# Attention weights moved in two transfers from 64 partitions to 128 rows in place of four from 32 to 64

## The chip, the cores and the metric

The kernel runs on one core of one Trainium2 chip. A time is the device time of one execution in microseconds, and the metric is the median over runs of the same kernel. Beside the runs there is one profiled execution, whose records give the durations used below.

## What is computed

The inputs are q, k and v of 8 batches, 8 heads, 576 positions and a head size of 64, a threshold `tau`, and the weights of a feed-forward layer. Everything is float32 for the attention; the feed-forward weights arrive as 64-bit floating-point values, which the kernel converts itself. Cut to what matters:

```python
scores = scale * np.matmul(q, k.transpose(0, 1, 3, 2))
thresh = np.max(scores, axis=-1, keepdims=True) - tau
scores = np.where(scores >= thresh, scores, -1000000000.0)
attn = softmax(scores)
x = np.matmul(attn, v)                      # then (B,H,S,D) -> (B*S, H*D)
h = x @ w_in
solu = h * softmax(h)
ln = (solu - mean(solu)) / np.sqrt(var(solu) + 1e-06) * g_ln
out = ln @ w_out
```

`x` has 4608 rows of 512, `h` 1024 columns.

## The kernel before

The work of the attention is cut into slots of 128 query rows for each of two heads. A slot is written (b, kind, hp, r): batch, kind, pair of heads, and half r. Kinds 0 and 1 are the two halves of the first 512 positions, kind 2 the last 64 positions of all four pairs. Two slots, r = 0 and r = 1, are a unit; there are 8 x 2 x 4 = 64 units of kinds 0 and 1 and 8 of kind 2, 72 in all, of 144 slots.

The program is one hand-written loop of rounds (L839 to L984), one slot a round, with an order for each engine that is exactly the order of the calls. In a round:

- TensorE makes the scores of the slot in PSUM, two heads side by side (`scores`, L451). VectorE takes the row minimum of the negated scores (`maxes`, L473), ScalarE applies threshold and exponential (`ramp` L488, `exps` L497), GpSimd normalises the rows one round later (`normalise`, L504 to L507).
- VectorE then transposes the weights in blocks of 32x32 into T (`blocks`, L519). The block of 32 query rows number R (0 to 3) of a slot lies in T's partitions 32 R to 32 R + 31, and a partition there stands for key position mod 32. T has two buffers.
- After the second slot of a unit SyncE's queue issues the block transfers (L530). They turn T into wT, where 64 partitions hold 64 key positions (the block column's half c is folded into the partition: source partition j gives target rows 2j and 2j + 1), so that TensorE can contract over keys. wT has two buffers and a part g of its free dimension.
- About three rounds later (`LAG_PV`, L750) TensorE multiplies v with wT: 72 matmuls a unit of kinds 0 and 1, on 64-row halves u of wT and of v (`attend_steps`, L555). ScalarE copies the sum from PSUM to xh, in the order of tokens (`attended`, L578).
- The feed-forward part of earlier tokens fills the rest of each round: `ff_h` (L611), `ff_max`, `ff_exp`, `ff_mul`, `ff_stats`, `ff_norm` and `ff_norm2` on the other engines, then `ff_swap` (four transfers V<-u on SyncE's queue, L693), the transpose `ff_turn` (L703), `ff_o` (L715) and the store (L742).

SyncE's queue carries nearly all transfers, in the order in which the round issues them: V<-u of `ff_swap` ahead of wT<-T, then stores, the transposed k (kT<-flip, L194), and last the loads of q, k, v and, in the first 16 rounds, of the weights (`weight_load`, L248). The weight pieces are converted on VectorE (L259 to L282), ScalarE (L264, L298) and GpSimd (L292) in those rounds too.

In the kernel before, the transfers of a unit pair the quarter R = 2 half + g with target rows 64 half to 64 half + 63 and part g, and so the half u of TensorE's rows is R // 2 and the part g is R % 2:

```python
for g in range(2):
    for half in range(2):
        of = 64 * half + 32 * g
        nc.sync.dma_start(out=to[ROWS[half], g], in_=T[of : of + 32])
```

Of the kernel before, what the change touches and what calls it, by code (L numbers as in the profile page):

```python
# [16 lines left out]
P = 128  # L17
# [3 lines left out]
def kernel(  # L21
# [27 lines left out]
    nc = tc.nc  # L49
# [10 lines left out]
    ROWS = (slice(0, 64), slice(64, P))  # L60
# [35 lines left out]
    xh = {}  # L96
# [414 lines left out]
    def blocks(s):  # L511
        b, kind, hp, r = slots[s]
        key = (b, kind, hp)
        if r == 0:
            units[key] = dict(T=work.tile([P, NB, 2, 2, 32], F32, tag="T", name="T"))
        u = units[key]
        T = u["T"]
        for h, w in enumerate(live.pop(s)["w"]):
            nc.vector.transpose(out=T[:, :, r, h, :], in_=w)  # L519
        if r == 0:  # L520
            return


        T = T.rearrange("p (c m) r h x -> p c (m r h x)", c=2)
        u["wT"] = wT = work.tile([P, 2, NK, 2, 2, 32], F32, tag="wT", bufs=2, name="wT")
        to = wT.rearrange("p g m r h x -> p g (m r h x)")
        for g in range(2):
            for half in range(2):
                of = 64 * half + 32 * g
                nc.sync.dma_start(out=to[ROWS[half], g], in_=T[of : of + 32])  # L530
# [31 lines left out]
    def attended(key):  # L562
        b, kind, hp = key
        tag, y = units.pop(key)["y"]
        y = y.rearrange("p (u n) -> p u n", u=2)[:, :, 0:P].rearrange("p u (r y) -> p u r y", r=2)
        if kind == 2:
            if b % 2 == 0:
                xe[b // 2] = work.tile([P, NP, P], F32, tag="xe", bufs=1, name="xe")
            to = xe[b // 2][:, :, 64 * (b % 2) : 64 * (b % 2) + 64].rearrange(
                "p (u r) y -> p u r y", u=2  # L570
            )
        else:
            if hp == 0:
                xh[b, kind] = work.tile(
                    [P, NP, 256], F32, tag=f"xh{(2 * b + kind) % 4}", bufs=1, name="xh"
                )
            to = xh[b, kind][:, hp].rearrange("p (r u y) -> p u r y", r=2, u=2)
        nc.scalar.copy(out=to, in_=y)  # L578
        pairs_free.append(tag)

# [181 lines left out]
    for i in range(NP, NPAIR):  # L762
        b, hp = divmod(i, NP)
# [27 lines left out]
    for i in range(2 * NP, NPAIR):  # L791
        b, hp = divmod(i, NP)
# [16 lines left out]
    with tc.manual_schedule():  # L809
# [29 lines left out]
        while True:  # L839
# [29 lines left out]
            if more:  # L869
# [3 lines left out]
                while preps and preps[0][0] <= rnd and preps[0][1] <= room:  # L873
                    _, n, make, _ = preps.pop(0)
# [80 lines left out]
            if attending is not None:  # L955
                for _ in beside or attend_steps(attending):
                    pass
                attended(attending)
                b, kind, hp = attending
                if kind == 2 and b % 2:  # L960
                    ready.append((rnd + 1, [(b // 2,)]))
                elif kind < 2 and hp == NP - 1:
                    ready.append((rnd + 1, [(b, kind, 0), (b, kind, 1)]))
            if rnd - 1 in live:
                blocks(rnd - 1)
# [6 lines left out]
            if rnd in pieces:  # L972
                x = pieces[rnd]
# [44 lines left out]
```

## Time and profile before

| | |
|---|---|
| median of 3 runs | 885.61 us (884.29 to 887.14) |
| profiled execution, its own time | 883.54 us |
| its span, first to last instruction | 881.8 us |
| granted TensorE clock, mean | 0.980 |
| TensorE busy | 835.4 us |
| wT<-T transfers | 288 of 288 KB, 5.9 us from issue to landing (median) |
| transfers in all | 161.60 MB, DMA engines busy 76.6% through SyncE's queue |
| eviction of pv to xh | 64 copies, 370 ns each |

The span is the time between the first and the last instruction of the program; 1.7 us of the execution lie outside it. The busy share of an engine is a mean over an opening, in which the weights are converted, a long middle of equal rounds, and an end in which only the feed-forward part runs.

### The profile page before, as it was taken

The page shows a single profiled execution, that of the slowest core. Times are in us where ns is not written, and L with a number is a line of the kernel's source. Part 1 is how long each engine was busy: PE and PEld are TensorE (multiplying, and loading weights), DVE is VectorE, ACT ScalarE, POOL GpSimd, SP SyncE. Part 2 cuts the span into 40 slices and gives each one's busy share as a digit, 9 for nine tenths or more (in the row PEclk, how much of TensorE's full clock was granted, in tenths as well). Part 3 has the DMA queues.
Part 4 walks back from the last instruction along what each step waited for, and adds up shares of the span by engine and source line. Part 5 has one row for each costly group of instructions (what it writes and reads, how often), then busy time and mean ns, then how long its engine had stood idle before and what let it go on. Part 6 is the DMA issues. An engine that isn't in the chain of part 4 may idle for free. (4 is left out here: it accounts for less than half of the span.)

```text
span 881.8 us, 38016 instructions
## 1 busy us (share of the span) xinstructions
PE 835.4 (95%) x16225; PEld 592.1 (67%) x16225; DVE 682.0 (77%) x1248; ACT 586.3 (66%) x1201; POOL 471.0 (53%) x888
## 2 busy tenths in 40 slices
PE   5667999989999999999999999999999999999997
PEld 3445666665676877677777777777677677777655
DVE  5989788878787888888778887888687888777451
ACT  5977777767666766767677677777676777775121
POOL 2878655545555555555554655555555555555120
PEclk9878899999999999999999999999999999999999
DMA  7999978887878796988789787888779777866222
GB/s 230 254 260 256 218 186 196 217 191 175 201 170 212 178 208 157 206 207 189 158 194 214 184 204 166 208 213 185 165 173 219 182 174 155 186 133 143 65 49 49
DMA packets 85033, 161.60 MB, mean 183 GB/s; under 512 B 19832, under 2 KB 49536, under 8 KB 84864
## 3 DMA queue, kind: packets, MB, share of 16 engines
q1 hardware_dynamic: 83728, 157.18, 76.6%
q8 instruction: 127, 2.08, 1.1%
q10 hardware_dynamic: 1136, 2.00, 0.7%
q14 instruction: 42, 0.34, 0.1%
HBM read 46.14 MB, written 9.44 MB: 63 GB/s over the span
## 5 line engine op out<-in xcount | busy, mean ns | idle before, releaser
L473 DVE CUSTOM_DVE_ANT_0 w<-s_ps,tau_t 128x576 f32<-128x576 f32 x280 | 200.7, 754 | 108.0 <-PE s_ps L451 90.7
L715 PE MATMUL o_ps<-w,uT 64*64 64x256 f32 x4608 | 265.2, 376 | 1.1 <-DVE uT L703 1.1
L488 ACT ACTIVATE w<-s_ps,nth 128x576 f32<-128x576 f32 x280 | 199.8, 743 | 97.0 <-DVE nth L473 93.1
L715 PEld LDWEIGHTS o_ps<-w,uT 64*64 64x64 f32 x4608 | 218.9, 133 | 58.3 <-issue 13.8
L507 POOL TENSOR_SCALAR w<-w,sm 128x576 f32<-128x576 f32 x288 | 218.8, 772 | 14.3
L497 ACT ACTIVATE w<-w,ntau 128x576 f32<-128x576 f32 x288 | 220.3, 772 | 0.0
L611 PE MATMUL h_ps<-w,xh 64*64 64x512 f32 x1856 | 220.0, 596 | 0.0
L519 DVE STREAM_TRANSPOSE T<-w 128x576 f32<-128x576 f32 x288 | 206.3, 752 | 7.4 <-POOL w L507 6.0
L555 PEld LDWEIGHTS pv<-wT,v 64*64 64x64 f32 x5760 | 166.5, 136 | 51.1 <-issue 36.3
L451 PE MATMUL s_ps<-kT,qT 64*64 64x64 f32 (+1 forms) x2048 | 168.1, 422 | 16.4 <-ACT w L488 12.5
L555 PE MATMUL pv<-wT,v 64*64 64x128 f32 (+1 forms) x5760 | 170.9, 263 | 7.9 <-DMA wT<-T 3.7
L611 PEld LDWEIGHTS h_ps<-w,xh 64*64 64x64 f32 x1856 | 98.3, 135 | 96.6 <-issue 88.6
L504 POOL TENSOR_SCALAR sm<-sm 128x2 f32<-128x2 f32 x144 | 36.0, 250 | 229.5 <-ACT w L497 226.4
L505 POOL TENSOR_TENSOR sm<-sm,mone 128x2 f32<-128x2 f32 x144 | 104.6, 726 | 12.0
L677 ACT ACTIVATE V<-u,nb,rs 128x1024 f32<-128x1024 f32 x36 | 44.7, 1241 | 52.2 <-POOL nb L667 52.2
L451 PEld LDWEIGHTS s_ps<-kT,qT 64*64 64x64 f32 x2048 | 61.8, 139 | 25.1 <-ACT w L488 17.7
L578 ACT COPY xh<-pv 128x256 f32<-128x256 f32 x64 | 23.7, 370 | 67.3 <-PE pv L555 67.3
L703 DVE STREAM_TRANSPOSE uT<-V 128x1024 f32<-128x1024 f32 x36 | 44.5, 1236 | 23.7 <-DMA V<-u 23.5
L497 ACT ACTIVATION_READ_ACCUMULATOR w<-w,ntau 128x1 f32 x288 | 56.9, 198 | 0.0
L635 ACT ACTIVATE u<-h_ps,hm 128x1024 f32<-128x1024 f32 x36 | 40.2, 1118 | 21.2 <-DVE hm L626 15.3
L626 DVE TENSOR_REDUCE hm<-h_ps 128x1 f32<-128x1024 f32 x36 | 43.1, 1197 | 12.2 <-PE h_ps L611 6.2
L682 DVE TENSOR_SCALAR u<-u,rs,nb 128x1024 f32<-128x1024 f32 x36 | 42.4, 1178 | 12.7 <-ACT V L677 12.4
(82 smaller groups left out, 590.4 us busy)
## 6 DMA issues: line engine op xcount, KB each, us to landing
wT<-T SPq DMA_DIRECT2D x288, 288.0 KB, 5.9
v<-in_v_dram SPq DMA_DIRECT2D x48, 288.0 KB, 4.8
V<-u SPq DMA_DIRECT2D x144, 64.0 KB, 4.1
out_dram<-ob SPq DMA_DIRECT2D x71, 128.0 KB, 3.1
q<-in_q_dram SPq DMA_DIRECT2D x15, 512.0 KB, 5.9
k<-in_k_dram SPq DMA_DIRECT2D x96, 72.0 KB, 4.6
kT<-flip SPq DMA_DIRECT2D x48, 144.0 KB, 2.7
raw<-in_moe_w_out_dram SPq DMA_DIRECT2D x8, 512.0 KB, 8.2
```

The lines of the kernel that those rows point to most:

```text
L451: nc.tensor.matmul(out=ps[h][ROWS[y], ks], lhsT=lhsT, rhs=d["kT"][ROWS[h], ks], start=True, stop=True,)
L473: nc.vector.tensor_tensor_reduce(out=w, in0=ps[:, 0:S], in1=(zero if loose else tau_t).to_broadcast([P, S]), scale=1.0, scalar=BIG, op0=AL ...
L488: nc.scalar.activation(out=d["w"][x], in_=d["w"][x] if d["loose"] else d["ps"][x][:, 0:S], func=AF.Prelu, bias=d["nth"][x], scale=-1.0, al ...
L497: nc.scalar.activation(out=w, in_=w, func=AF.Exp, bias=ntau, scale=1.0, accum_out=sm[:, x : x + 1])
L505: nc.gpsimd.tensor_tensor(out=sm, in0=sm, in1=mone, op=ALU.pow)
L507: nc.gpsimd.tensor_scalar(out=w, in0=w, scalar1=sm[:, x : x + 1], scalar2=1.0, op0=ALU.mult, op1=ALU.mult)
L519: nc.vector.transpose(out=T[:, :, r, h, :], in_=w)
L555: nc.tensor.matmul(out=to, lhsT=d["v"][ROWS[u], h0 + h, m ^ 4 * u if m < 8 and b < 2 else m], rhs=rhs, start=m == 0, stop=m == NK - 1,)
L611: mm = nc.tensor.matmul(out=h[ROWS[y], f], lhsT=x[ROWS[r], c, ROWS[y]], rhs=w1_parts[ROWS[r], c, part ^ r], start=part == 0 and c == 0, st ...
L677: nc.scalar.activation(out=V, in_=u, func=AF.Identity, bias=nb, scale=rs)
L703: nc.vector.transpose(out=uT, in_=d["V"].rearrange("p y (m x) -> p m y x", x=32))
L715: nc.tensor.matmul(out=d["o"][ROWS[z], 512 * r : 512 * r + 256], lhsT=d["uT"][ROWS[r], m].rearrange("p y x -> p (y x)"), rhs=w2[ROWS[r], m ...
```

## The change

For units of kinds 0 and 1, the four block transfers become two. Each takes 64 partitions of T (two quarters R) and writes all 128 rows of one part g of wT. The pairing of quarters changes with it: now R = 2 g + u, so that part g is R // 2 and the half u of the rows is R % 2. The matmuls of `attend_steps` stay as they are, but what they leave in PSUM has its tokens in another order, and the copy to xh puts them right with runs of 32 elements where it had runs of 64. Units of kind 2 keep their four transfers and their copy.

```diff
         for g in range(2):
+            if kind < 2:
+                nc.sync.dma_start(out=to[:, g], in_=T[ROWS[g]])
+                continue
             for half in range(2):
                 of = 64 * half + 32 * g
                 nc.sync.dma_start(out=to[ROWS[half], g], in_=T[of : of + 32])
...
         tag, y = units.pop(key)["y"]
-        y = y.rearrange("p (u n) -> p u n", u=2)[:, :, 0:P].rearrange("p u (r y) -> p u r y", r=2)
+        y = y.rearrange("p (u n) -> p u n", u=2)[:, :, 0:P]
         if kind == 2:
+            y = y.rearrange("p u (r y) -> p u r y", r=2)
...
-            to = xh[b, kind][:, hp].rearrange("p (r u y) -> p u r y", r=2, u=2)
+            y = y.rearrange("p u (rg x) -> p u rg x", x=32)
+            to = xh[b, kind][:, hp].rearrange("p (rg u x) -> p u rg x", u=2, x=32)
         nc.scalar.copy(out=to, in_=y)
```

In the kernel after, the new transfers are line L529, the kept ones L533, the matmuls L558 and the copy L583.

## The prediction

> **What bounds the kernel now.** I read the busy times of the engines first, then the busy times by stretch, then the waits of TensorE, then the DMA issues and SyncE's timeline. The page opens with
>
> ```profile
> span 881.8 us, 38016 instructions
> PE 835.4 (95%) x16225; PEld 592.1 (67%) x16225; DVE 682.0 (77%) x1248; ACT 586.3 (66%) x1201; POOL 471.0 (53%) x888
> ```
>
> TensorE is busy for 835.4 of 881.8 us: whatever the change does to other engines or to the transfers can gain only from the 46.4 us that are left, unless it shortens a matmul, and it touches none (same operand shapes, same count). The table by stretch says where those 46.4 us lie (length, then busy us of PE, PEld, DVE, ACT, POOL, then granted clock, DMA share, GB/s):
>
> ```profile
> 0.00:40.00 40.00, 25.33 (x473) 16.39 (x473) 28.67 (x65) 28.71 (x66) 21.48 (x37) 0.91 0.87 244
> 40.00:80.00 40.00, 29.72 (x464) 21.47 (x464) 36.13 (x73) 29.13 (x61) 30.65 (x39) 0.83 1.04 257
> 80.00:120.00 40.00, 33.62 (x692) 23.36 (x688) 31.32 (x63) 31.37 (x72) 27.80 (x45) 0.87 0.93 223
> ...
> 500.00:600.00 100.00, 100.00 (x2037) 71.06 (x2033) 81.51 (x148) 70.03 (x145) 54.52 (x106) 1.00 0.85 199
> ```
>
> The first 120 us leave TensorE idle for 14.7 + 10.3 + 6.4 = 31.4 us, with VectorE near full in 40 to 80 (36.1 of 40) and the DMA engines full (1.04, 0.93). Later TensorE is full and the DMA share of 0.85 has cover. So the change has to be paid in the opening, or by the few stalls afterwards. Who ended TensorE's waits:
>
> ```profile
> PE s_ps L451 <- ACT w L488: 12.5, 14, 2.8
> PE tp L318 <- DMA k<-in_k_dram: 6.0, 1, 6.0
> PE pv L555 <- DMA wT<-T: 3.7, 6, 1.3
> ```
>
> (Each line: total us, times, longest.) The transfers that are changed cost TensorE 3.7 us in 6 waits: 2.3 us in 3 waits before 125 us, 1.4 us in 3 after 200. Of VectorE's waits between 40 and 100 us these two count here:
>
> ```profile
> DVE em L259 <- DMA raw<-in_moe_w_out_dram: 1.6, 1, 1.6
> ...
> DVE em L259 <- DMA raw<-in_moe_w_in_dram: 0.5, 1, 0.5
> ```
>
> It waits 2.1 us for weight loads, which SyncE issues right behind wT. The transfers themselves, and SyncE's work on two units in mid-kernel:
>
> ```profile
> wT<-T SPq DMA_DIRECT2D x288, 288.0 KB, 5.9
> ...
> kT<-flip SPq DMA_DIRECT2D x48, 144.0 KB, 2.7
> ```
>
> ```profile
> 405.25 3.49 SPq L530 DMA_DIRECT2D wT<-T  x4
> 409.20 3.37 SPq L693 DMA_DIRECT2D V<-u  x4
> ```
>
> A unit is four issues in 3.5 us; each lands 5.9 us after its own issue, the unit's last about 8.4 us after the first (median over the units, from the issues whose landing is recorded).
>
> [...] The trace of before has a transfer of the new form, kT<-flip (64 partitions to 128 rows): its 1152-byte packets take 81.5 ns on average, 14.1 bytes per ns, and wT's 4608-byte packets 327 ns, also 14.1. [...] the trace decides, and I take the rate as unchanged. [...] about 16 packets are in flight in mid-burst. [...] half-clock stretches of 3.4, 6.8 and 10.2 us before 100 us. [...]
>
> **The change, part by part.** (1) Removed: two of four issues in each of 64 units (8 batches, 2 kinds, 4 pairs); the 8 kind-2 units keep four. 288 issues become 64 x 2 + 8 x 4 = 160. At a median 0.62 us SyncE gets 128 x 0.62 = 79 us back. SyncE sets no end itself: it waits 113.6 us for VectorE's T alone, so the 79 us are worth nothing directly. I take an issue of the new size at the old duration; the loads to 128 rows take 0.33 to 1.0 us, so it lies within 0.3 us of that. (2) The bytes and the packets (4608 bytes each) stay: 256 issues x 64 packets = 128 x 128. At an equal rate the DMA engines' 377 us of wT packets (summed, over 16) stay. Bounds: [...] packets could fall towards the uncontended 178 ns, at most 377 x 149 / 327 x 64/72 = 153 us less DMA time[...]. I take zero and keep both ends. (3) Landing: the last issue comes about 0.7 us after the first instead of about 2.9. Where the queue is already full (the unit at 405.25: packets flow without a break from 407.7 to 413) that changes nothing; where it starts empty (417.34) it can give up to 2.2 us. I take 0.8 us, between 0 and 2.2. (4) TensorE's waits on wT: 0.2, 1.3 and 0.7 (one unit, 63.9 and 65.0), then 0.2, 1.1 and 0.2 us. Minus 0.8 for each unit: 0.2 + 0.8 + 0.2 + 0.8 + 0.2 = 2.2 us less, of 3.7. The 63.9 one is on the path: the next scores stand behind these matmuls on TensorE, and VectorE waits for them. (5) SyncE's next instructions (weight load, V<-u, stores, loads of q, k, v) leave about 1.3 us earlier for each unit. In the opening that meets 2.1 us of VectorE's waits; as the DMA engines are full there, I count a quarter, 0.5 us. In mid-kernel it meets VectorE's 23.5 us of waits for V<-u, which TensorE's full queue covers; counted at nothing. Were this cover gone, VectorE's 20% of slack would still take it. (6) Eviction (L578): the same 64 copies of 128x256, in runs of 32 instead of 64 elements. 370 ns each; bounds below nothing excluded, since nothing is dropped, up to 100 ns more, 6.4 us on ScalarE, which is 66% busy. Next on TensorE is a wait of o_ps weight loads for this copy, 0.5 us at most and hidden under running matmuls. Taken at nothing. (7) No wait is added: the first pv matmuls needed two transfers, now they need both of the two; VectorE rewrites T two units later, far behind. A kind-2 unit is as before.
>
> Sum: 2.2 + 0.5 = 2.7 us. What is late next is VectorE and ScalarE in the opening (12.5 us of TensorE's waits for ACT w), which the change doesn't touch. The profiled execution took 883.54 us, 1.7 more than its span, and lies 2.1 us under the median of the three runs (885.61); taken off the median, 885.6 - 2.7 = 882.9.
>
> **The rivals.** A, [...] the opening is DMA-full at 1.04, so weight loads come earlier as well. Against: kT<-flip's equal rate. Then all 3.7 us of waits and the 2.1 us on weight loads go, minus a little that turns into waits for VectorE: about 5.5 us, with one half-clock stretch of 3.4 us (worth 1.7) perhaps avoided: 879.5. B, hidden anyway: landing is set by the queue's throughput, which stays, and the opening by VectorE. For: the packets of 407.7 to 413 without a break, VectorE's 36.1 of 40. Then 0 to 0.5 us: 885.3. C, the slower one: [...] as both transfers must be there before the first pv matmul. Place: the pv waits in mid-kernel. About a dozen of the 72 units land under 1 us before their first pv matmul or after it; their shortfalls add up to about 3 us of stalls for 0.5 us of delay and 8 us for 1 us. It decides from 0.5 us of later landing on (a unit's 5 us of packets 10% longer, with no help from the issues), and at 0.7 us it costs about 4.6 and gives 890. Against it: the issues come earlier. That the change doesn't do what it says is not a case: the order of instructions shows L529 with 128x1x1152 twice where four stood, and nothing else moved.
>
> **How the numbers follow.** Forecast (882.9, its own range 881.0 to 885.2): 0.45. A: 0.25. B: 0.13. C: 0.17. About 0.3%, 2.7 us, is what a measurement of this kernel can tell from no change: under 882.9 is faster, over 888.3 slower. The forecast stands on that bound: half of its chance is faster, 0.23, half the same, 0.22. A is faster. B is the same. C is slower but for 0.02 between. So 0.48 faster, 0.37 same, 0.15 slower. The range takes in most of A and the lower part of C: 878.5 to 888.5.
>
> **What would show it.** 160 wT issues, with a median to landing of 6 to 7.5 us for the double size; under 5.5 speaks for A, over 8 for C. TensorE's waits for wT fall from 3.7 to about 1.5 us. wT's packets stay at 310 to 340 ns. The eviction stays at 370 ns. TensorE's busy time stays near 835. Wrong would be: more waits of pv for wT, a changed rate of the packets, or opening stretches that move by more than 3 us through the clock alone.

## The result and the profile after

The changed kernel takes 889.41 us (median of 22 runs, 885.95 to 897.86), the kernel before 885.83 (22 runs, 879.95 to 892.93): a ratio of 1.0061, 95% interval 1.0034 to 1.0089. It is slower, by 3.6 us between the medians and 5.4 us between the means, where 2.7 us less had been forecast, and it lies just outside the range of 878.5 to 888.5. All ratios here are of means, and leave out runs over 1.5% above the fastest of their own kernel (4 of 17 in e0_after, 1 of 6 in e10_spaced). The profiled execution of after is the longest of its 22 (897.86 us, against 883.54 for the profile of before), so the two profiles lie 14.3 us apart and sums over the trace of after are larger than those of a usual run.

The page after, at the places that were shown of before: span, busy times, TensorE's instruction queue (queue: packets, MB, share), eviction, transfers.

```profile
span 896.1 us, 37760 instructions
...
PE 840.1 (94%) x16225; PEld 601.7 (67%) x16225; DVE 681.1 (76%) x1248; ACT 587.2 (66%) x1201; POOL 471.9 (53%) x888
...
q8 instruction: 127, 2.08, 1.0%
...
L583 ACT COPY xh<-pv 128x256 f32<-128x256 f32 x64 | 23.7, 371 | 71.3 <-PE pv L558 71.2
...
wT<-T SPq DMA_DIRECT2D x128, 576.0 KB, 7.2
...
wT<-T SPq DMA_DIRECT2D x32, 288.0 KB, 6.1
```

The parts that were priced came out near their prices: 160 issues, the copy at 371 ns, the double transfer landing 7.2 us after its issue. From the first issue of a unit to its last landing it is 8.5 us where it was 9.0 (medians of the 64 units of kinds 0 and 1), and a wT packet takes 324 ns where it took 327. Yet TensorE is 14.3 us longer under way: 4.7 us more busy (840.1 for 835.4) and 9.7 us more idle (gaps of 44.9 for 35.2). The waits of TensorE say in what:

```profile
PE s_ps L451 <- ACT w L488: 12.3, 14, 2.8
PE tp L318 <- DMA k<-in_k_dram: 6.0, 1, 6.0
PE pv L558 <- DMA wT<-T: 4.7, 4, 2.3
PE pv L558 <- issue: 4.5, 3, 3.3
PE s_ps L318 <- ACT w L488: 3.4, 3, 2.5
PE s_ps L451 <- issue: 2.8, 1, 2.8
PE o_ps L720 <- issue: 2.7, 3, 2.0
...
PE s_ps L318 <- issue: 1.2, 1, 1.2
```

Four lines of "issue", 11.2 us in 8 stalls, in which TensorE waited for nothing that the program knows. Before had 2.2 us in 4:

```profile
PE pv L555 <- issue: 1.3, 2, 1.0
...
PE s_ps L451 <- issue: 0.5, 1, 0.5
PE h_ps L611 <- issue: 0.5, 1, 0.5
```

These stalls alone are 9.0 of the 9.7 us. Waits for ACT w and for k are as they were, and the wait for wT didn't fall. By stretch (length, busy us of PE, PEld, DVE, ACT, POOL, clock, DMA share, GB/s), first before, then after:

```profile
400.00:500.00 100.00, 99.35 (x2004) 70.70 (x2000) 81.57 (x149) 70.54 (x143) 55.88 (x110) 1.00 0.81 187
600.00:700.00 100.00, 98.36 (x1955) 70.01 (x1951) 79.94 (x147) 69.14 (x140) 55.53 (x109) 1.00 0.79 181
```

```profile
400.00:500.00 100.00, 96.04 (x1889) 64.72 (x1885) 76.01 (x140) 65.77 (x135) 51.52 (x100) 0.97 0.77 179
600.00:700.00 100.00, 96.22 (x1915) 71.16 (x1910) 75.28 (x135) 64.87 (x134) 50.23 (x99) 0.97 0.75 175
```

Every engine does less in the same time: 1889 matmuls for 2004. The loss is in mid-kernel, where TensorE had been full. Set against the same matmul of before, after is 0.5 us late at 119 us and 0.0 at 404, then 6.3 late at 440, 7.5 at 628, 12.3 at 665 and 14.4 at the end: two steps make most of it. The first, on TensorE's timeline (start, length, operation), before and after:

```profile
433.10 0.91 PE L555 MATMUL pv<-wT,v 64*64 64x64 f32 x46
433.80 0.23 PE L451 MATMUL s_ps<-kT,qT 64*64 64x64 f32 x2
...
433.86 1.19 PE L451 MATMUL s_ps<-kT,qT 64*64 64x64 f32 x14
```

```profile
433.10 0.47 PE L558 MATMUL pv<-wT,v 64*64 64x64 f32 x15
436.89 1.13 PE L558 MATMUL pv<-wT,v 64*64 64x64 f32 x33 [3.32 <-issue]
437.80 2.14 PE L451 MATMUL s_ps<-kT,qT 64*64 64x64 f32 x16
```

In the middle of a run of pv matmuls, of which the profile shows no wait for an operand, TensorE stops for 3.32 us. Then it runs at half clock: the 16 scores take 2.14 us where the same 16 took 1.25 before (433.80 to 435.05). In all it is at half clock for 52.8 us, before for 36.8; two stretches of 6.8 us begin at 435.7 and 643.9 us, at the two longest stalls. TensorE does 36.9 us of its work at half clock where it did 27.9; as the trace gives the granted clock there as 0.5 of full, half of the difference, 4.5 us, is what it costs: an estimate, and nearly all of the 4.7 us more of busy time.

**What the stops have in common.** TensorE stops at instruction 15809 here and at 24001 in the second step (644.72 us, 2.81 us). The 8 stalls of this profile stand at TensorE's instruction number 193 or 194 modulo 256, all of them. The trace also records the packets of the queue that the page calls instruction (q8): 127 of 16384 bytes. TensorE has some 32,600 instructions (a weight load and a matmul for each of the 16225, and its waits), which makes about 256 to a packet. Each stall ends 1.2 to 1.7 us after the end of such a packet (435.63 and 643.40 us for these two). The stalls, the packets and the count of instructions fit blocks of 256 instructions, one packet each. By count few boundaries matter, as 8 of 126 show a stall here, but these 8 cost 11.2 us.

So a cause offered itself after the result: TensorE's next block arrives late. Between TensorE's start on a block and the start of the next packet the median is 1.2 us before and 1.5 after, the 95th percentile 3.1 and 4.4. Why later was the question for the experiments. SyncE now puts a whole unit on its queue in 1.2 us:

```profile
405.24 1.18 SPq L529 DMA_DIRECT2D wT<-T  x2
```

Before, the four issues at this place took 3.49 us. Two forms of the theory were held against each other: **B**, the packet stands behind all that is queued when it comes (two runs of 36 KB to each of the 16 DMA engines within 1.2 us); **F**, it stands behind the run of a single transfer, which doubled from 18 to 36 KB to an engine. What one engine gets is an estimate here and below: the 288 or 576 KB of a transfer in equal shares over the 16 engines that the page counts. The rivals without fetch were the new pairing of quarters (what is read and written at the same time) and the eviction.

### The profile page after: what moved, and what is told of

Read it like the earlier page. It is cut to its first block, busy times and chain, and to the rows that moved or that the text cites. A ratio compares the mean times of both kernels' runs of the same rounds, so it can differ in the third digit from the quotient of the medians.

```text
span 896.1 us, 37760 instructions
## 1 busy us (share of the span) xinstructions
PE 840.1 (94%) x16225; PEld 601.7 (67%) x16225; DVE 681.1 (76%) x1248; ACT 587.2 (66%) x1201; POOL 471.9 (53%) x888
## 5 line engine op out<-in xcount | busy, mean ns | idle before, releaser
L720 PE MATMUL o_ps<-w,uT 64*64 64x256 f32 x4608 | 269.9, 376 | 3.6 <-issue 2.7
L507 POOL TENSOR_SCALAR w<-w,sm 128x576 f32<-128x576 f32 x288 | 218.5, 772 | 14.3
L616 PE MATMUL h_ps<-w,xh 64*64 64x512 f32 x1856 | 224.9, 598 | 0.1
L558 PEld LDWEIGHTS pv<-wT,v 64*64 64x64 f32 x5760 | 170.1, 136 | 50.9 <-issue 31.9
L451 PE MATMUL s_ps<-kT,qT 64*64 64x64 f32 (+1 forms) x2048 | 174.2, 426 | 16.9 <-ACT w L488 12.3
L558 PE MATMUL pv<-wT,v 64*64 64x128 f32 (+1 forms) x5760 | 172.6, 263 | 12.3 <-DMA wT<-T 4.7
L616 PEld LDWEIGHTS h_ps<-w,xh 64*64 64x64 f32 x1856 | 106.2, 136 | 94.0 <-issue 73.1
L504 POOL TENSOR_SCALAR sm<-sm 128x2 f32<-128x2 f32 x144 | 36.8, 256 | 239.0 <-ACT w L497 236.0
L451 PEld LDWEIGHTS s_ps<-kT,qT 64*64 64x64 f32 x2048 | 65.7, 139 | 26.1 <-ACT w L488 17.5
L583 ACT COPY xh<-pv 128x256 f32<-128x256 f32 x64 | 23.7, 371 | 71.3 <-PE pv L558 71.2
L646 DVE TENSOR_TENSOR u<-h_ps,u 128x1024 f32<-128x1024 f32 x36 | 42.8, 1189 | 11.2 <-ACT u L640 11.2
```

The source lines that it names most:

```text
L451: nc.tensor.matmul(out=ps[h][ROWS[y], ks], lhsT=lhsT, rhs=d["kT"][ROWS[h], ks], start=True, stop=True,)
L507: nc.gpsimd.tensor_scalar(out=w, in0=w, scalar1=sm[:, x : x + 1], scalar2=1.0, op0=ALU.mult, op1=ALU.mult)
L558: nc.tensor.matmul(out=to, lhsT=d["v"][ROWS[u], h0 + h, m ^ 4 * u if m < 8 and b < 2 else m], rhs=rhs, start=m == 0, stop=m == NK - 1,)
L616: mm = nc.tensor.matmul(out=h[ROWS[y], f], lhsT=x[ROWS[r], c, ROWS[y]], rhs=w1_parts[ROWS[r], c, part ^ r], start=part == 0 and c == 0, st ...
L720: nc.tensor.matmul(out=d["o"][ROWS[z], 512 * r : 512 * r + 256], lhsT=d["uT"][ROWS[r], m].rearrange("p y x -> p (y x)"), rhs=w2[ROWS[r], m ...
```

## Experiments

Edits are against the changed kernel unless another is named. In the expectations on record the fetch delays 1.9 and 2.7 us are called medians; they are upper quartiles (the medians are 1.2 and 1.5). The table has, from one profiled execution each, TensorE's stalls that end in "issue", its waits for wT, the 90th percentile of the time from the start of a block to the next fetch between 200 and 800 us, the time from a unit's first issue to its last landing, and the time of its issues.

| kernel | ratio to before (95%) | issue stalls, us | wT waits, us | fetch, us | landing, us | issues, us |
|---|---|---|---|---|---|---|
| before | 1 | 2.2 | 3.7 | 2.8 | 9.0 | 3.6 |
| after | 1.0061 (1.0034 to 1.0089) | 11.2 | 4.7 | 3.5 | 8.5 | 1.2 |
| e0_after | 1.0050 (1.0023 to 1.0077) | 14.0 | 4.9 | 3.5 | 8.7 | 1.2 |
| e1_map4 | 1.0088 (1.0061 to 1.0116) | 3.4 | 5.8 | 2.6 | 9.3 | 4.5 |
| e7_map4_alt | 1.0051 (1.0028 to 1.0074) | 3.6 | 5.1 | 2.5 | 9.4 | 3.6 |
| e9_evict32 | 0.9982 (0.9955 to 1.0008) | 1.9 | 5.6 | 2.7 | 9.1 | 3.6 |
| e2_cols | 0.9978 (0.9958 to 0.9998) | 2.8 | 3.9 | 2.2 | 8.2 | 3.7 |
| e8_cols3 | 0.9977 (0.9954 to 1.0000) | 2.5 | 4.6 | 2.0 | 8.2 | 4.8 |
| e3_old8 | 1.0109 (1.0075 to 1.0144) | 0.2 | 3.9 | 1.8 | 9.0 | 5.7 |
| e6_cols_alt | 0.9918 (0.9885 to 0.9951) | 4.3 | 0.9 | 2.4 | 8.2 | 3.7 |
| e10_spaced | 1.0672 (1.0618 to 1.0725) | 7.6 | 27.4 | 3.1 | 9.7 | 5.1 |
| e11_spaced1 | 1.0009 (0.9981 to 1.0037) | 1.1 | 4.2 | 3.1 | 8.5 | 3.6 |

The wT waits of e9, which has the old transfers, are 5.6 us where before has 3.7: differences of 2 us in that column are not read.

**The change again** (e0_after), unaltered.

> The changed kernel once more, as the yardstick of this call. Theory F (instruction fetch): TensorE's instructions come in blocks of 16384 bytes (256 instructions) through the same DMA engines; the transfer of 128 rows gives each DMA engine a run of 8 packets of 4608 bytes in place of 4, and the fetch stands behind it, so that TensorE stops at block boundaries. It expects 0.3 to 0.9% over the kernel before, the fetch packet of a block starting 2.7 us (median) after the block before it began to run (1.9 in the kernel before), and 5 to 12 us of TensorE idle time that ends in issue. Theory P [...]: the loss comes from wT landing later; it expects more waits of pv for wT in the middle of the kernel. Theory C (chance of the opening): within 0.2% of before.

Measured: 891.61 us over all 17 runs, 888.61 over the 13 that the ratio counts, for 884.38. Its profiled execution is again its longest (901.05 us), so it is used for where the stalls stand, not for how much they cost. Its 9 stalls stand again at 193 or 194 modulo 256, but at other blocks in part. That makes 17 of 17, and such a stall is no property of one place in the program.

**The new pairing with four transfers** (e1_map4), from 32 to 64 partitions as before.

```diff
-                nc.sync.dma_start(out=to[:, g], in_=T[ROWS[g]])
+                for half in range(2):
+                    of = 64 * g + 32 * half
+                    nc.sync.dma_start(out=to[ROWS[half], g], in_=T[of : of + 32])
```

> The new pairing of quarters and the new eviction in runs of 32, but four transfers from 32 partitions to 64 rows as before. Theory F expects the time of the kernel before, 0.998 to 1.002, and a median fetch delay of 1.9 us. A rival that blames the eviction or the permuted rows expects the loss of 0.6% to stay. Theory P expects the time of before too.

Measured: 892.09 us, 1.0088, where theory F had expected no loss. The issue stalls are down to 3.4 us (in a profile of 889.31 us, one of its shorter runs), but the kernel is no faster. So the pairing has a price of its own when it is carried by the small transfers: packets of 340 ns instead of 327, landing 9.3 instead of 9.0 us. The profile ends 5.8 us later than that of before; 1.5 us of this come at one stall of 2.5 us (640 us), where before has one of 1.0, and the rest gathers slowly.

**The new transfers in column halves** (e2_cols): 64 to 128 rows, four of 288 KB.

```diff
-                nc.sync.dma_start(out=to[:, g], in_=T[ROWS[g]])
+                for c in (slice(0, 576), slice(576, 1152)):
+                    nc.sync.dma_start(out=to[:, g, c], in_=T[ROWS[g], :, c])
```

> 64 partitions to 128 rows as in the change, but each transfer cut into two halves of the columns: four issues a unit, 8 packets of 2304 bytes for each DMA engine, 18 KB in a run as before the change. Theory F expects the loss to go: 0.997 to 1.002 of before, median fetch delay about 1.9 us. Theory P [...] expects the loss to stay, 1.004 to 1.008[...].

Measured: 882.89 us for 884.38, 0.9978. Same rows, same pairing, same eviction as the change, with four issues again in 3.7 us: stalls 2.8 us, and the loss is gone. B and F both allow it: a unit is queued over a longer time, and the run of a transfer is halved.

**The old transfers in column halves** (e3_old8), against the kernel before: eight issues a unit.

```diff
-                nc.sync.dma_start(out=to[ROWS[half], g], in_=T[of : of + 32])
+                for c in (slice(0, 576), slice(576, 1152)):
+                    nc.sync.dma_start(out=to[ROWS[half], g, c], in_=T[of : of + 32, :, c])
```

> The kernel before with each of its four transfers cut into two halves of the columns: eight issues a unit, 4 packets of 2304 bytes for each DMA engine, 9 KB in a run. Theory F expects a median fetch delay under 1.9 us, about 1.5, fewer stalls at block boundaries, and a time at or under that of before, 0.994 to 1.001, unless eight issues (about 5 us of SyncE for each unit) make wT land later, which would show as waits of pv for wT. Theory P expects no gain, 1.000 to 1.006.

Measured: 893.68 us, 1.0109, with only 0.2 us of issue stalls. TensorE waits elsewhere, 4.34 us at once for qT at 182.6 us and 1.6 for a load of q; that these come late because of SyncE's eight issues (5.7 us a unit) is likely and not shown. Both theories had expected less. Fewer fetch stalls and yet slower: few stalls don't make a kernel fast.

**Halves taken in turn, with the large rows** (e6_cols_alt): the first columns of both parts go first.

```diff
-        for g in range(2):
-            if kind < 2:
-                nc.sync.dma_start(out=to[:, g], in_=T[ROWS[g]])
-                continue
+        if kind < 2:
+            for c in (slice(0, 640), slice(640, 1152)):
+                for g in range(2):
+                    nc.sync.dma_start(out=to[:, g, c], in_=T[ROWS[g], :, c])
+        for g in range(2) if kind == 2 else ():
```

> 64 partitions to 128 rows in halves of the columns (640 and 512), the column halves outermost, so that the two source halves of 64 partitions alternate and the first key blocks of both parts land with the first two transfers. Theory F (a DMA engine's run of one transfer holds back TensorE's instruction blocks; 20 KB in a run here, 18 in the kernel before, 36 in the change): stalls of TensorE at block boundaries as in the kernel before, 0 to 4 us. Theory P [...]: landing of the last transfer at or under 8.1 us after the first issue, and a time at or under that of the version in column halves, 0.993 to 0.999 of before.

Measured: 879.18 us for 885.66, 0.9918, faster than both kernels. Of TensorE's waits in e6:

```profile
PE pv L559 <- issue: 2.7, 2, 1.7
...
PE s_ps L318 <- issue: 1.6, 1, 1.6
...
PE pv L559 <- DMA wT<-T: 0.9, 2, 0.6
```

The waits for wT fall to 0.9 us. A pv matmul of an early key block needs both parts of that block only, and these now land with the first two transfers (the transfers of 320 KB land 4.6 us after their issue, the change's of 576 KB after 7.2). TensorE is 3.7 us ahead of before at 101 us, 5.4 at 404 and 3.1 at the end. So the waits that the prediction wanted to shorten can be shortened, by the order of the columns. That this is the whole gain isn't shown: the means are 7.3 us apart (0.9918 of 885.7) and the profiles 3.0, and in the profile TensorE is 5.8 us less busy than before (829.7 for 835.4) and not less idle.

**The pairing with its halves in turn** (e7_map4_alt).

```diff
-        for g in range(2):
-            if kind < 2:
-                nc.sync.dma_start(out=to[:, g], in_=T[ROWS[g]])
-                continue
+        if kind < 2:
+            for g, half in ((0, 0), (1, 1), (0, 1), (1, 0)):
+                of = 64 * g + 32 * half
+                nc.sync.dma_start(out=to[ROWS[half], g], in_=T[of : of + 32])
+        for g in range(2) if kind == 2 else ():
```

> The new pairing of quarters with four transfers of 32 to 64, in the order that alternates the source halves and the target halves, as the kernel before does: (0,0), (1,1), (0,1), (1,0). Theory P expects the loss of the four transfers in the plain order (1.009 of before) to go, 0.998 to 1.003, with the last landing back near 9.0 us from 9.3. A rival that blames the eviction in runs of 32 or the pairing itself, sources in one half and targets in the other, expects it to stay, 1.006 to 1.011.

Measured: 890.19 us for 885.66, 1.0051; theory P had expected no loss. The interval overlaps with e1's: that e1 reads its two transfers from one half in a row explains at most part of the pairing's price. Packets stay at 340 ns. Longer packets alone can't be the price, as e11 below has packets of 343 ns and no such loss.

**Thirds** (e8_cols3), six issues.

```diff
-        for g in range(2):
-            if kind < 2:
-                nc.sync.dma_start(out=to[:, g], in_=T[ROWS[g]])
-                continue
+        if kind < 2:
+            for g in range(2):
+                for c in range(0, 1152, 384):
+                    nc.sync.dma_start(out=to[:, g, c : c + 384], in_=T[ROWS[g], :, c : c + 384])
+        for g in range(2) if kind == 2 else ():
```

> 64 partitions to 128 rows in thirds of the columns: six issues a unit, 8 packets of 1536 bytes for each DMA engine, 12 KB in a run. Theory F expects the fetch delays in the middle of the kernel (90th percentile 3.5 us in the change, 2.7 before, 2.2 with halves, 1.8 with 9 KB runs) to fall to about 2.0 us, and stalls at block boundaries under 3 us in sum. If SyncE's six issues cost nothing, 0.994 to 1.000 of before; if SyncE is what limits then, up to 1.008 with later V<-u.

Measured: 0.9977, as e2. Halving was enough; a third cut takes the fetch delay from 2.2 to 2.0 us and gives nothing more.

**The eviction alone** (e9_evict32), against the kernel before: same transfers, the copy in runs of 32.

```diff
-        y = y.rearrange("p (u n) -> p u n", u=2)[:, :, 0:P].rearrange("p u (r y) -> p u r y", r=2)
+        y = y.rearrange("p (u n) -> p u n", u=2)[:, :, 0:P]
         if kind == 2:
+            y = y.rearrange("p u (r y) -> p u r y", r=2)
...
-            to = xh[b, kind][:, hp].rearrange("p (r u y) -> p u r y", r=2, u=2)
+            y = y.rearrange("p u (r g x) -> p u g r x", r=2, g=2)
+            to = xh[b, kind][:, hp].rearrange("p (r u g x) -> p u g r x", r=2, u=2, g=2)
```

> The kernel before with only its eviction rewritten: the same elements go to the same places, in runs of 32 instead of 64 elements. Theories F and B (both about transfers) expect 0.998 to 1.002 of before. A rival that blames the eviction for the loss of the new pairing with four transfers (1.005 to 1.009) expects 1.004 or more.

```profile
L580 ACT COPY xh<-pv 128x256 f32<-128x256 f32 x64 | 23.7, 370 | 63.6 <-PE pv L555 63.6
```

370 ns for a copy, ratio 0.9982 with 1 inside its interval: the eviction costs nothing. It is out.

**The change, with its two transfers held apart** (e10_spaced): three transfers of 64 bytes between them, into a tile that nothing reads.

```diff
                 nc.sync.dma_start(out=to[:, g], in_=T[ROWS[g]])
+                for x in range(3 if g == 0 else 0):
+                    nc.sync.dma_start(out=pad[0:16, x : x + 1], in_=mhalf[0:16])
```

> The change as it is, with three transfers of 64 bytes in all, to a tile that nothing reads, between the two transfers of each unit: the second leaves SyncE about 2.3 us after the first instead of 0.6. Theory B (TensorE's instruction blocks wait for what is queued at their DMA engine at that moment; the change queues a whole unit at once, four issues spread it) expects the stalls at block boundaries to fall from 11 to 14 us to under 5, the 90th percentile of the fetch delay from 3.5 to under 2.9 us, and the time from 1.005 to 0.997 to 1.002 of before. Theory F in its first form (the run of 8 x 4608 bytes of a single transfer holds the block back) expects stalls of 8 us or more and a time of 1.004 or more.

```profile
407.52 0.74 SPq L530 DMA_DIRECT2D wT<-T  x1
408.30 3.48 SPq L532 DMA_DIRECT2D pad<-mhalf  x3
411.82 0.59 SPq L530 DMA_DIRECT2D wT<-T  x1
```

Measured: 941.4 us, 1.0672. An overshoot: the spacers take 3.48 us, the second transfer leaves 4.3 us after the first, and TensorE waits 27.4 us for wT. Of the 7.6 us of issue stalls, 1.7 us are at block boundaries, as theory B expected (the others stand elsewhere and are not explained), but its time and its fetch delay (3.1 us where under 2.9 was expected) missed. The run says little of the price, and a smaller dose follows:

**One spacer** (e11_spaced1), `range(1 if g == 0 else 0)` in place of `range(3 if g == 0 else 0)`.

> The change with one transfer of 64 bytes (to a tile that nothing reads) between the two of each unit, in place of three, so that the second leaves about 1.8 us after the first and wT lands at most 0.6 us later than in the change. Theory B expects stalls at block boundaries between those of the change (11 to 14 us) and those of four issues (2 to 4 us), about 7, a 90th percentile of the fetch delay in the middle of the kernel of 3.2 us or less (3.5 in the change), and a time at or under that of the change, 0.998 to 1.005 of before, as long as TensorE's waits for wT stay under 6 us. Theory F expects the stalls and the time of the change, 1.005 or more. Waits for wT well over 6 us would say that SyncE's time is the dearer of the two.

```profile
407.03 0.53 SPq L530 DMA_DIRECT2D wT<-T  x1
407.61 0.60 SPq L532 DMA_DIRECT2D pad<-mhalf  x1
408.25 2.31 SPq L530 DMA_DIRECT2D wT<-T  x1
```

The unit's issues take 3.6 us again, as before. Measured: 886.05 us for 885.44, 1.0009, issue stalls 1.1 us (7 had been expected). Both transfers keep their rows, their size, their pairing and their run of 36 KB. What has changed is when SyncE queues the second one, and with it all that follows on SyncE's queue; the run doesn't separate these two. The loss is gone, or at most 0.37% by the interval: inside the kernel this speaks for B and against F.

Whether a whole unit lies queued can be counted in the traces. At each block of instructions that TensorE enters between 150 and 800 us (98 to 102 in a kernel) one takes the wT packets whose issue is done and which have not landed (a unit has 256), and the time to the start of the next fetch:

| | before | e9 | e1 | e7 | after | e0 | e11 |
|---|---|---|---|---|---|---|---|
| blocks entered with 192 packets or more queued | 1 | 1 | 1 | 0 | 14 | 13 | 0 |
| blocks whose next fetch starts over 3.5 us later | 1 | 1 | 3 | 2 | 12 | 10 | 5 |

In after the fetch starts 0.9 us later on average when none is queued, 1.9 us with 1 to 191, and 3.0 us with 192 or more. The two long stalls follow blocks that were entered with 210 and 187 packets queued. This fits B, and it sets e1 and e7 apart: they lose time with a queue like that of before, so their loss has another cause.

The limits: the fetch's 90th percentile falls only from 3.5 to 3.1 us in e11, and 15 of its blocks still arrive under 1.8 us before TensorE runs them (17 in after, 8 in before), so that another execution of e11 can have more stalls; each count is one execution's.

**Bare chains.** Four kernels leave out the whole computation: 8192 calls of an fp32 matmul of 64x64 by 64x128 without waits (16384 matmuls and 16384 weight loads in the trace, so 128 blocks of 256 instructions), beside them SyncE's stream of 90 units (`UNITS`) as fast as it goes. m0_none has no stream, m1_run36 the change's two transfers, m2_run18c the column halves of e2 with the parts in turn, m3_run18 the four old ones.

```diff
+        for n in range(UNITS):
+            wT = work.tile([P, 2, 1152], F32, tag="wT", bufs=4, name="wT")
+            for g in range(2):
+                nc.sync.dma_start(out=wT[:, g], in_=T[ROWS[g]])
```

> Only a chain of 8192 matmuls (64x64 weights, 128 columns) that wait for nothing, and one store of zeros at the end; attention and feed-forward are left out, and no transfers run beside the chain. Both theories expect TensorE without idle time over 0.15 us once it runs, about 30 ns for each matmul, 250 us in all: the base of the three others.

> The same chain beside 90 units of block transfers in the form of the change (64 partitions to 128 rows, two a unit, runs of 8 x 4608 bytes for each DMA engine); attention and feed-forward are left out. Theory F expects idle time of TensorE at every second or third block of 256 instructions, the most of the three streams, with the fetch packet starting 1 us or more later than in the other two. A rival, that any stream of the same bytes delays the blocks alike, expects the three streams to be equal within 10%.

> As the one before, each transfer cut into two halves of the columns (four a unit, runs of 8 x 2304 bytes). Theory F expects clearly less idle time of TensorE at block boundaries than with runs of 36 KB, by a third or more, and about as much as with four transfers from 32 to 64. The rival expects the same idle time as with 36 KB.

> As the one before, the stream in the form of the kernel before (32 partitions to 64 rows, four a unit, runs of 4 x 4608 bytes). Theory F expects the idle time of the version in halves, within 30%[...]. The rival expects the idle time of all streams to be equal.

| | time, us | issue stalls, us (count) | fetch delay under load, us (median, 90th percentile) | unit, first issue to last landing, us | wT packets queued on average, in units |
|---|---|---|---|---|---|
| m0_none | 477.98 | 9.6 (10) | 1.1, 1.4 (no stream) | | |
| m1_run36 | 720.42 | 188.5 (61) | 5.6, 5.7 | 18.9 | 2.4 |
| m2_run18c | 686.29 | 162.4 (62) | 5.1, 5.3 | 12.1 | |
| m3_run18 | 719.61 | 184.3 (57) | 5.7, 5.9 | 13.4 | 1.0 |

Here is the mechanism alone: matmuls that depend on nothing lose 188.5 us to a stream that they have nothing to do with, and all of it at one instruction number modulo 256. But m1 and m3 are alike, though a transfer's run is 36 KB in one and 18 in the other: F falls. (m2 loses 14% less, in a stream that is 7% shorter.) B in its simplest form falls with it, since m1 has more than twice as much queued as m3 and no later fetch. The fetch is held up by 4.0 to 4.6 us (the medians less m0's 1.1) beside a queue that is always full, whatever stands behind (2.4 units on average in m1, 1.0 in m3). At the 241 to 265 GB/s of these runs an engine moves 66 to 69 KB in that time (an estimate): about 15 packets of 4608 bytes in m1 and m3, about 29 of m2's 2304 bytes. Since a transfer puts 8 packets on an engine in m1 and 4 in m3, this reaches over several transfers, whatever their length. What sets this amount was not shown. A unit is 74 KB to an engine (73,728 bytes).

**Chains with a pace.** Again only bare matmuls, now of 64x256, with ScalarE's copies meant to set the pace of 140 units so that the DMA engines have time to spare. m5_paced2 queues both transfers of a unit together, m6_spread2 the same two a copy (2.1 us) apart, m7_paced4 four of 32 to 64 together.

```diff
-    nc.scalar.copy(out=spare, in_=fill)
-    nc.scalar.copy(out=T, in_=fill)
     for g in range(2):
+        nc.scalar.copy(out=T[ROWS[g]], in_=fill[ROWS[g]])
         nc.sync.dma_start(out=wT[:, g], in_=T[ROWS[g]])
```

The diff is m5 to m6; m7 is m5 with the loop of e1 over `half`, its parts as in the kernel before.

> A chain of matmuls (64x64 weights, 256 columns) beside 140 units of block transfers, which a chain of copies on ScalarE paces; attention and feed-forward are left out. The two transfers of 64 to 128 rows of a unit follow each other, as in the change. Theory B (what is queued at once) expects a 90th percentile of the time from the start of one block of 256 instructions to the start of the next fetch packet of 3.5 to 5 us, well above that of the spread form. Theory F (length of the run) expects the same delay as in the spread form, within 0.4 us.

> The same chain, bytes, transfers and ScalarE copies, but the two transfers of a unit are released one copy (about 2.7 us) apart. Theory B expects the 90th percentile of the fetch delay at least 1 us under that of the two in a row. Theory F expects it equal within 0.4 us, as the runs of 8 x 4608 bytes are the same.

> The same chain and pace with four transfers of 32 to 64 rows a unit, released together, so that SyncE's own issue time spreads them. Both theories expect less delay than with two in a row; B because the issues take about 2.4 to 3.6 us, F because the runs are of 4 x 4608 bytes. F expects the lowest delay of the three here, B one between the two others or equal to the spread form.

They took 985.61, 916.60 and 993.65 us. Their issue waits, m5, m6 and m7 in this order:

```profile
PE acc L78 <- issue: 74.9, 62, 2.1
```

```profile
PE acc L76 <- issue: 21.5, 22, 1.5
```

```profile
PE acc L80 <- issue: 85.5, 74, 1.8
```

The same bytes and the same transfers at nearly the same period (4.70 and 4.79 us) cost 21.5 us when held apart, 74.9 together. The median time from a block's start to the next fetch is 5.5, 2.7 and 5.6 us. But the pace was too fast for a clean comparison: the copies took 2.1 us where 2.7 had been counted on. ScalarE waited 48 times (20.8 us) in m5 and 103 times (38.9 us) in m7 for wT to land, in m6 only twice (1.4 us). So m5 and m7 ran at what the DMA engines could carry, with the periods of m1 and m3 (m5 4.70 for 4.71 us, m7 4.90 for 4.88), and m6 just under it; part of the difference between m5 and m6 is that of a queue that never empties. m7 missed both expectations: SyncE's four issues spread its unit over 3.5 us, as in the kernel before, and it had the most stalls. The three runs show that the fetch is late where the queue stays full, however the unit is cut. That spreading a unit helps rests on e11 in the kernel, and not on these.

## Why the prediction was wrong

By its own steps:

1. **"SyncE sets no end itself ... the 79 us are worth nothing directly"** is the step that failed. The 79 us did come free (a unit's issues take 1.2 us for 3.6), and were worth less than nothing: SyncE's slow issue had kept a unit from lying queued as a whole (blocks of instructions entered with 192 wT packets or more queued: 1 before, 14 after), and so left room for a user of the DMA engines that the prediction didn't have on its list, TensorE's own instructions. The profile of before shows it, as a queue of its own (packets, MB, share):

```profile
q8 instruction: 127, 2.08, 1.1%
```

A share that small was passed over, though what counts of it is when each packet comes. Price: 9.0 us of stalls more in the profiled execution, and with the half clock (4.5 us more, the estimate above) some 14 us; over 22 runs 5.4 us between the means for everything. e11 gives it from the other side: with SyncE made to spend the time again, 1.0061 becomes 1.0009.

2. Rate of the packets taken as unchanged: right, 324 ns for 327, far from the bound of 178 (a quarter of the wT packets of before took no more than 179 ns).
3. Landing 0.8 us earlier: right in direction, 0.5 us measured (9.0 to 8.5; the prediction's 8.4 us for before came from a part of the units). The queue that it took as already full at 405.25 us wasn't: no packet was under way at 406.0, and the unit's first one started at 406.4, not at 407.7.
4. Waits for wT from 3.7 to 1.5 us: wrong, 4.7 and 4.9. In the opening they rose from 2.3 to 3.8, later they fell from 1.4 to 0.9. Since e9 has 5.6 with the old transfers, one profile doesn't carry a step of 2.2 us in this row. e6 points to what was missing: a pv matmul waits for both parts of its key block, and two large transfers in a row bring part 0 whole before the first block of part 1. The prediction's sentence that "now they need both of the two" had this, and gave it no price.
5. Weight loads earlier: VectorE's waits on them fell from 2.1 to 0.8 us, but TensorE is 0.5 us late at 119 us, not early. Nothing of the 0.5 us counted shows.
6. Eviction at nothing: right, 371 ns, and e9 as a kernel.
7. "No wait is added": true of the program, whose semaphores gained none. A wait that no instruction states was added all the same.

Of the rivals, A (packets shortened to about 250 ns) didn't come: 324. B's reason, that landing is set by the queue's throughput, was half right (0.5 us), and its time wrong. C gave the right side by luck, with the wrong mechanism: it had the unit land later, but it landed earlier, and the stalls of pv are not for wT but for instructions. Of the signs listed beforehand, 160 issues, 7.2 us to landing, 324 ns and 371 ns fitted the forecast; the waits for wT and TensorE's busy time (840.1, not near 835) did not.

**What is settled and what is not.** Shown: the stalls are late instruction blocks (17 of 17 at boundaries); they come with a unit that lies queued at once (the count of queued packets, and e11, where only SyncE's issue time is as long as before and the loss is gone); they don't come from run length (m1 and m3, e11) or from the eviction (e9). Not shown: how much a usual execution of the change loses to them, as both of its profiles are of long executions. Shown too, but not explained: the new pairing costs 0.5 to 0.9% with four transfers of 32 to 64 partitions (e1, e7), with 3.4 and 3.6 us of issue stalls. With the transfers of 64 to 128 rows, spaced or cut, that loss isn't there (e11 1.0009, e2 0.9978). Why it is the pairing of source and target halves that should matter stays open, and so does the split of the change's 0.6% between this and the fetch; that e2 also halves the packets (2304 bytes) leaves open how much of its gain is spacing. Why some blocks are hit and others spared in one execution was not traced; with 17 of 126 blocks arriving under 1.8 us before they were needed, against 8 in before, small shifts may decide it.

## What to carry to other kernels

Transfers queued all at once can stop a full TensorE that waits for none of them (here 8 stalls, 11.2 us, for 4 with 2.2 us before): before merging DMA issues or clearing the queue that issues them, look for the engine's instruction queue in the page, and read "issue" stalls at equal distances in instructions (here 256) as late code, not as late data. If a merge is wanted, try cutting it so that the first consumer's data comes first (e6: 0.9918, its gain not fully explained) or keep something between the parts (e11: 1.0009). A queue's issue time that "costs nothing" (here 3.6 us a unit) may be doing work as a spacer.

## What the runs showed of the hardware that was not expected

- With no stream beside the chain (m0) the fetch packet starts 1.1 us (90th percentile 1.4) after TensorE enters the block before, takes 1.05 us, and at a stall the first instruction runs 1.3 to 1.6 us after its end: 3.5 to 4.0 us for a block of 256 instructions, an estimate from these sums. TensorE used a block up in 3.7 us (478 us for 128 blocks), and had 9.6 us of stalls in 10 places, 7.7 of them in the first 40 us, where the store of 9216 KB runs (the DMA engines about 50 and 90% busy from 12 to 36 us). No idle time had been expected, and 250 us in all where it took 478: the 30 ns a matmul came near (28 ns, 464.2 us for 16384), but a call is two matmuls in the trace.
- Beside a full queue the fetch is late by about 4.5 us (medians of 5.6 and 5.7 us in m1 and m3 for m0's 1.1), the same for runs of 36 and of 18 KB and with 2.4 or 1.0 units queued; the latest fetch in m1 started after 6.3 us.
- The issue of a transfer itself can wait: in e11 the second 576 KB transfer, behind the first and a spacer, took 2.31 us to issue, the first 0.53.
- Saturated, the stream of m1 (64 to 128 rows) took 432.7 us, that of m3 (32 to 64) 442.4, that of m2 (column halves, the parts in turn) 402.6: twice the written rows gave 2%, the cut and its order 7% more.
